# Silu and multiply kept in PSUM for the last tiles, adds on GpSimd, and GpSimd's and VectorE's remainders set apart in the load stage

## The chip, the cores and the metric

The kernel runs on one core of a Trainium2 chip. The metric is the time of the device in microseconds (us), the median of several runs; less is better. The profile is of one execution of the program. Its engines are PE (TensorE: matmuls, with PEld for its weight loads), DVE (VectorE), ACT (ScalarE), POOL (GpSimd) and SP, which here only issues DMAs.

## The reference

The input x has 2048 rows of 576. Two branches start from it and meet in the output.

```python
xn = _layernorm(x)
s  = A(xn)                 # linear attention, 32 heads of 18, hedgehog feature map
g  = _silu(B(xn))          # (silu(xn @ w_gate) * (xn @ w_up)) @ w_down, 4608 wide
return x + s * g
```

In A, q, k and v are xn times parts of `wqkv`; q and k are multiplied by `w_phi` per head and go through two softmaxes each (of the product and of its negative); `phi_k^T v` is summed over all rows, and each row of `phi_q` is multiplied by it, divided by its denominator and projected by `wo`. Everything is float32.

## The kernel before, in words

**Number format.** PE multiplies in a rounded 32-bit format (`F32R`). To keep accuracy, each operand is split in two: ACT rounds it (`hi`), and a subtraction gives the remainder (`lo = src - hi`). A product is then three matmuls, hi by hi, hi by lo, lo by hi. The width 576 is 4 x 128 + 64; the last 64 are kept as two tails of 32, each laid out so that the remainder of the tail lies in other partitions of the same tile as its rounded part. For x it is in partitions 32 to 63, for weights in 64 to 95; one matmul with 96 rows then does all three products of a tail. `split_rows` (L63) makes such a split of a weight: an ACT copy, a DVE subtraction for the two full chunks (L65) and a second one for the tail (L66).

**The load stage** (about the first 67 us) loads x in four blocks of 512 rows, in the order 2, 3, 0, 1. `norm_stats` (L179) takes mean and variance on DVE, with a square root on ACT. `norm_block` (L195) normalises the four 128-row pieces in turn on DVE (L201) and ACT (L198, collected in `norms`), copies the tails on POOL (L204), transposes on PE (L213), rounds the result into the `X` tiles on ACT (L215, L220) and subtracts for the remainders: the full chunks on DVE (L216), the two tails on POOL (L223), from a copy `xr` in SBUF (ACT, L221). `xr` also goes to DRAM from ACT's queue (L224). `fold` (L235) multiplies wk and later wq by w_phi on PE (L242) and splits the result into `KVWH`/`KVWL` and `QH`/`QL`. w_v comes in six chunks `wv[n]` with k = n // 3 and c = n % 3: ACT rounds each (L274), POOL subtracts for the four with c < 2 (L276, 128 x 576), DVE for the two tails c = 2 (L278, 32 x 576). The tiles `wst` that hold wk's five groups, w_v's six chunks and wq's five groups share five buffers, so SP's load of a later one waits until the one five places before it has been used. In between, `early_weights` (L102) splits the first weights of the feed-forward branch (ahead of other work, by `tc.high_priority()`) and `early_tile` (L119) computes gate and up products for the blocks that are ready, as work for PE: two PSUM banks `pe`, silu on ACT (L126), multiply on DVE (L130), store to DRAM, here from POOL's queue (L131).

**The middle** is k, v and the sums over rows, then q and the projection, then for both halves of the rows the feed-forward branch, whose gate and up products (L741) and down products (L866) are done by a seven-product scheme; `combine` (L1022) puts its sums together. For the first half the result goes to `y_dram` and is finished along the way (`late_finish`).

**The end** is `plain(1, ...)` (L869): the last two of the 36 column blocks of the feed-forward branch, added to the sums in `acc`, for the eight tiles of 128 rows of the second half, in the order 4, 5, 6, 7, 0, 1, 2, 3. For each tile `tile_of` (L882) fills a PSUM tile from `acc` on ACT (L893), adds 12 matmuls in two half widths of 288 (L866), and `finish` (L834) does silu on ACT into `acc` (L837), the multiply by s on DVE (L838), the add of x (L839) on DVE for even tiles and on POOL for odd ones, and the DMA to the output on SP (L840). s and x of two tiles at a time are loaded by `final_rows` (L854). Seven tiles use the two buffers `pd`, of two PSUM banks each; the last one, tile 3 (`fine`), uses the banks `py` and `pw`, one for each half, and finishes each half by itself, all on DVE. The other two banks, `px`, belong to the gate and up products and are idle here. So all eight banks are spoken for.

**What sets the order.** A scheduler orders each engine's instructions when the program is built: by their place in the text, by `tc.high_priority()`, and by its own model of when inputs are ready. `tc.issue_after(ins)` queues the instructions of a block behind `ins` in the queue of its engine. The engines work their queues in order.

Of the kernel before, what the change touches and what calls it, by code (L numbers as in the profile page):

```python
# [9 lines left out]
F32 = mybir.dt.float32  # L10
# [8 lines left out]
P = 128  # L19
# [29 lines left out]
def gated_hedgehog_kernel(ctx: ExitStack, tc, x, w_qk, w_v, w_phi, wo, w_gu, w_tail, w_down, ident_in, mask_in, out):  # L49
# [13 lines left out]
    def split_rows(hi, lo, src):  # L63
        nc.scalar.copy(hi, src)
        nc.vector.tensor_sub(lo, src[:, :, 0:2], hi[:, :, 0:2])  # L65
        nc.vector.tensor_sub(hi[64:96, :, 2], src[64:96, :, 2], hi[64:96, :, 2])  # L66
# [34 lines left out]

    def early_weights(f, *behind):  # L102
        parts = []
        for m in (0, 2):
            raw = epool.tile([P, 2, 3, P], F32, name="raw", bufs=2)
            hi = epool.tile([P, 2, 3, P], F32R, name="wh", bufs=3)
            lo = epool.tile([P, 2, 2, P], F32R, name="wl", bufs=3)
            nc.sync.dma_start(raw, w_gu[f, :, m:m + 2])
            with ExitStack() as order:
                for b in behind:  # L110
                    order.enter_context(tc.issue_after(b.ins))
                with tc.high_priority():
                    split_rows(hi, lo, raw)
            parts.append((hi, lo))
        return parts
# [19 lines left out]
    with ExitStack() as att:  # L135
# [17 lines left out]
        with ExitStack() as wst:  # L153
# [4 lines left out]
            with ExitStack() as pst:  # L158
# [36 lines left out]
                def norm_block(b, xns):  # L195
# [12 lines left out]
                    for c in range(3):  # L208
# [13 lines left out]
                        for m in range(2):  # L222
                            nc.gpsimd.tensor_sub(dst[m][32:64, 2], xr[32:64, m], dst[m][32:64, 2])  # L223
                            nc.scalar.dma_start(x_dram[i, :, :, 2 * j + m].rearrange("s p n -> p s n"),  # L224
                                                xr[:, m].rearrange("p (s n) -> p s n", s=4))
# [39 lines left out]
                wv = []  # L265
                for n in range(6):
                    wv.append(prep.tile([P, 6 * P], F32, name="wst", bufs=5))
                    nc.sync.dma_start(wv[n][:, 0:D], w_v[:, n // 3, n % 3])
                xns = load_x(0) + load_x(1)
                for n in range(6):  # L270
                    k, c = divmod(n, 3)
                    src, vh = wv[n][:, 0:D], KVWH[:, k, c, D:2 * D]
                    with tc.issue_after(copy.ins):
                        nc.scalar.copy(vh, src)  # L274
                    if c < 2:
                        nc.gpsimd.tensor_sub(KVWL[:, k, c, D:2 * D], src, vh)  # L276
                    else:
                        nc.vector.tensor_sub(vh[64:96], src[64:96], vh[64:96])  # L278
                wq = load_fold(1)
                norm_stats([0, 1], xns)  # L280
                norm_block(0, xns[0:4])
# [552 lines left out]
    def finish(t, k, pd, sx, eng):  # L834
        r0 = HS + t * P
        a = acc[:, t // 4 * 2:t // 4 * 2 + 2, t % 4][:, k]
        nc.scalar.activation(a, pd, AF.Silu)  # L837
        nc.vector.tensor_mul(a, a, halves_of(sx[:, 0])[:, k])  # L838
# [30 lines left out]
    def plain(i, fs, hr, final):  # L869
# [11 lines left out]

        def tile_of(t, hs):  # L882
            fine = i == 1 and t == HT // 2 - 1
            if fine:
                pd = [fps.tile([P, BT], F32, name=n, bufs=1)[:, 0:HALF] for n in ("py", "pw")]
            else:
                both = fps.tile([P, 2, 512], F32, name="pd", bufs=2)[:, :, 0:HALF]
                pd = [both[:, k] for k in range(2)]
            c = slice(t % 4 * P, t % 4 * P + P)
            a2 = acc[:, t // 4 * 2:t // 4 * 2 + 2, t % 4]  # L890
            with tc.high_priority() if i else ExitStack():
                for k in range(2 if fine else 1):
                    nc.scalar.copy(pd[k] if fine else both, a2[:, k] if fine else a2)  # L893
            for k in range(2):
# [3 lines left out]
                if fine:  # L898
                    finish(t, k, pd[k], final[t // 2][:, t % 2], nc.vector)
# [3 lines left out]
            elif not fine:  # L903
                finish(t, slice(0, 2), both, final[t // 2][:, t % 2], (nc.vector, nc.gpsimd)[t % 2])
# [250 lines left out]
```

## Time and profile before

| what | us |
|---|---|
| median of 3 runs (1623.53 to 1623.86) | 1623.55 |
| the profiled execution, its own time | 1622.04 |
| its span, first to last instruction | 1620.2 |
| PE busy in the span | 1605.8 (99%) |
| DVE busy | 1175.9 (73%) |
| ACT busy | 726.3 (45%) |
| POOL busy | 660.8 (41%) |

A row of the timeline gives the start in us from the span's beginning, how long the group took, the engine, the line of the kernel, the operation, what it writes and what it reads, the shape (partitions x elements) and how many instructions are merged in it; a bracket at the end says how long the engine had been idle before and what ended that. A row of a table by stage gives the stretch, its length, and for PE, PEld, DVE, ACT and POOL the busy time and the number of instructions; behind them stand the granted clock of PE, the share of DMA and GB/s. A row of the chain has start, length, engine, tile and line.

### The profile page before, as it was taken

The page shows a single profiled execution, that of the slowest core. Times are in us where ns is not written, and L with a number is a line of the kernel's source. Part 1 is how long each engine was busy: PE and PEld are TensorE (multiplying, and loading weights), DVE is VectorE, ACT ScalarE, POOL GpSimd, SP SyncE. Part 2 cuts the span into 40 slices and gives each one's busy share as a digit, 9 for nine tenths or more (in the row PEclk, how much of TensorE's full clock was granted, in tenths as well). Part 3 has the DMA queues.
Part 4 walks back from the last instruction along what each step waited for, and adds up shares of the span by engine and source line. Part 5 has one row for each costly group of instructions (what it writes and reads, how often), then busy time and mean ns, then how long its engine had stood idle before and what let it go on. Part 6 is the DMA issues. An engine that isn't in the chain of part 4 may idle for free.

```text
span 1620.2 us, 25277 instructions
## 1 busy us (share of the span) xinstructions
PE 1605.8 (99%) x9411; PEld 1428.2 (88%) x9412; DVE 1175.9 (73%) x1727; ACT 726.3 (45%) x1399; POOL 660.8 (41%) x710
## 2 busy tenths in 40 slices
PE   9999999999999999999999999999999999999998
PEld 6899998999988888888888888888888888888887
DVE  7777769898856778877777778634667656666578
ACT  5633345544445654444444444454343333333334
POOL 3676652334115635644535435223324314133132
PEclk9999999999999999999999999999999999999999
DMA  9522243436347454555545453965445654555435
GB/s 325 172 80 82 98 144 105 125 105 191 121 158 255 165 180 163 175 171 181 177 169 191 168 188 114 335 210 148 151 137 154 187 174 157 177 181 175 142 116 176
DMA packets 121420, 268.28 MB, mean 166 GB/s; under 512 B 12754, under 2 KB 53842, under 8 KB 119506
## 3 DMA queue, kind: packets, MB, share of 16 engines
q1 hardware_dynamic: 105852, 244.73, 45.9%
q0 software_dynamic: 3552, 12.59, 2.7%
q10 hardware_dynamic: 11894, 9.35, 1.8%
q8 instruction: 74, 1.21, 0.3%
q14 instruction: 48, 0.39, 0.1%
HBM read 167.53 MB, written 99.09 MB: 165 GB/s over the span
## 4 chain that ended last, share of the span: by engine, by line
PE 94%; DVE 3%; DMA 1%; ACT 1%; issue 0%; POOL 0%; SPq 0%; POOLq 0%; ACTq 0%
PE pd L866 25%; PE px L741 25%; PE pw L741 12%; PE p L94 7%; PE py L741 6%; PE pe L94 5%; PE p L641 4%; PE kvp L320 2%; PE po L621 2%; PE vx L408 1%; PE pt L615 1%; PE vw L408 1%; PE vy L94 1%; PE vx L94 1%; DVE stats L183 1%
## 5 line engine op out<-in xcount | busy, mean ns | idle before, releaser
L866 PEld LDWEIGHTS pd<-dw,hh 128*128 128x128 f32 x3036 | 431.0, 188 | 22.3 <-DVE X L997 0.9
L866 PE MATMUL pd<-dw,hh 128*128 128x288 f32 x3036 | 446.7, 297 | 0.7 <-DVE X L997 0.4
L741 PE MATMUL px<-X,w 128*128 128x512 f32 x1512 | 390.4, 393 | 0.0
L741 PEld LDWEIGHTS px<-X,w 128*128 128x128 f32 x1512 | 275.0, 188 | 52.7 <-ACT s L770 2.2
L741 PE MATMUL pw<-X,w 128*128 128x512 f32 x744 | 191.8, 393 | 0.0
L741 PEld LDWEIGHTS pw<-X,w 128*128 128x128 f32 x744 | 139.2, 189 | 30.9
L775 DVE TENSOR_TENSOR s<-pw,s 128x512 f32<-128x512 f32 x126 | 86.5, 688 | 101.0 <-ACT s L770 89.5
L997 DVE TENSOR_TENSOR acc<-pd,acc 128x576 f32<-128x576 f32 x128 | 96.2, 752 | 84.4 <-PE pd L866 84.2
L770 ACT COPY s<-px 128x512 f32<-128x512 f32 x126 | 73.9, 586 | 160.6 <-PE px L741 160.6
L61 DVE TENSOR_TENSOR hh<-ha,hh 128x512 fp32r<-128x512 f32 x140 | 111.9, 825 | 22.8 <-ACT hh L60 21.3
L60 ACT CAST hh<-ha 128x512 fp32r<-128x512 f32 x140 | 82.7, 619 | 87.0 <-PE pd L866 72.0
L969 POOL TENSOR_TENSOR hb<-hb 128x512 f32<-128x512 f32 x34 | 46.5, 1367 | 164.9 <-DVE hb L787 159.2
L94 PE MATMUL pe<-X,wh 128*128 128x512 f32 (+1 forms) x340 | 108.5, 399 | 1.9 <-POOL X L223 0.8
L61 DVE TENSOR_TENSOR w<-ld,w 128x512 fp32r<-128x512 f32 (+1 forms) x96 | 80.2, 835 | 36.6 <-ACT w L60 35.3
L741 PE MATMUL px<-X,wt 96*128 96x512 f32 x252 | 99.5, 395 | 0.0
L741 PE MATMUL py<-X,w 128*128 128x512 f32 x378 | 98.0, 394 | 0.0
L956 POOL TENSOR_TENSOR h<-ha,hb 128x512 f32<-128x512 f32 x34 | 44.4, 1305 | 125.1 <-DVE ha L791 95.2
L982 POOL TENSOR_TENSOR ha<-ha 128x512 f32<-128x512 f32 x34 | 52.6, 1563 | 98.7 <-DVE hh L61 98.7
L60 ACT CAST w<-ld 128x512 fp32r<-128x512 f32 (+1 forms) x96 | 52.7, 549 | 88.1 <-POOL ld L729 56.4
L795 ACT COPY py<-px 128x512 f32<-128x512 f32 x63 | 36.0, 572 | 106.4 <-PE px L741 83.4
L726 POOL TENSOR_TENSOR ts<-ld 128x256 f32<-128x256 f32 x32 | 27.4, 856 | 129.4 <-issue 73.3
L741 PEld LDWEIGHTS py<-X,w 128*128 128x128 f32 x378 | 67.8, 188 | 11.3
(275 smaller groups left out, 3249.2 us busy)
## 6 DMA issues: line engine op xcount, KB each, us to landing
w_dram<-w SPq DMA_DIRECT2D x90, 512.0 KB
w<-w_dram SPq DMA_DIRECT2D x90, 512.0 KB
wt<-t_dram SPq DMA_DIRECT2D x62, 336.0 KB
ld<-in_B_w_gu SPq DMA_DIRECT2D x32, 512.0 KB
X<-sum_dram SPq DMA_DIRECT2D x8, 1280.0 KB
rt<-in_B_w_down SPq DMA_DIRECT2D x33, 288.0 KB
rb<-in_B_w_down SPq DMA_DIRECT2D x33, 288.0 KB
w_dram<-w SPq DMA_DIRECT2D x30, 256.0 KB
```

What stands on the lines that cost most here:

```text
L60: nc.scalar.copy(hi, src)
L61: nc.vector.tensor_sub(lo, src, hi)
L94: last = nc.tensor.matmul(ps, l, r, start=n == 0, stop=n == len(pairs) - 1)
L641: nc.tensor.matmul(ps[:, 0:HALF], a[0:w, g, jc], bw[0:w, g, n], start=k == 0, stop=k == 3 * NG - 1)
L741: nc.tensor.matmul(ps, l, r, start=first and n == 0, stop=last and n == len(mm) - 1, skip_group_check=True)
L770: snaps.append(nc.scalar.copy(t, ps))
L775: nc.vector.tensor_add(t, ps, t)
L866: nc.tensor.matmul(ps, l, r, start=first and n == 0 and m == 0, stop=n == len(hs) - 1 and m == 2, skip_group_check=True)
L956: sub(s, g["h"][0][0], g["h"][0][1])
L969: nc.gpsimd.tensor_add(a21, a21, g["h"][1][1])
L982: sub(a12, a12, g["h"][0][0])
L997: nc.vector.tensor_add(a2, pd[:, :, 0:HALF], a2)
```

## The change

There are two parts.

In the load stage the two tail remainders of block 3 (the second block loaded) move from POOL to DVE with high priority and read PSUM. w_v's chunks are loaded and treated in another order: the four with c < 2 first, their POOL subtractions under `issue_after` of the last subtraction of the early weights (`rests[-1]`); the two tails c = 2 come in the text only behind the norms of block 0, their DVE subtractions under `issue_after` of `norms[5]`. The load of wq comes behind them in the text.

At the end `finish` is cut in two. `scaled` does the silu within PSUM and multiplies from PSUM into `acc`; `finish` adds x and stores. The adds go to POOL for all tiles but the last. Tiles 6 and 1 (`apart`) use the two `px` banks, one for each half, and are multiplied, added and stored by halves. For those two and the last tile, the fills are queued behind the tile before's, and the adds behind the second half's multiply.

```diff
     def split_rows(hi, lo, src):
...
-        nc.vector.tensor_sub(hi[64:96, :, 2], src[64:96, :, 2], hi[64:96, :, 2])
+        return nc.vector.tensor_sub(hi[64:96, :, 2], src[64:96, :, 2], hi[64:96, :, 2])
...
+    rests = []
+
     def early_weights(f, *behind):
...
-                    split_rows(hi, lo, raw)
+                    rests.append(split_rows(hi, lo, raw))
...
                         for m in range(2):
-                            nc.gpsimd.tensor_sub(dst[m][32:64, 2], xr[32:64, m], dst[m][32:64, 2])
+                            if b == 3:
+                                with tc.high_priority():
+                                    nc.vector.tensor_sub(dst[m][32:64, 2], ps[32:64, m], dst[m][32:64, 2])
+                            else:
+                                nc.gpsimd.tensor_sub(dst[m][32:64, 2], xr[32:64, m], dst[m][32:64, 2])
...
-                wv = []
-                for n in range(6):
-                    wv.append(prep.tile([P, 6 * P], F32, name="wst", bufs=5))
-                    nc.sync.dma_start(wv[n][:, 0:D], w_v[:, n // 3, n % 3])
+                wv, places = [], [(0, 0), (0, 1), (1, 0), (1, 1), (0, 2), (1, 2)]
+                for k, c in places:
+                    wv.append(prep.tile([P, 6 * P], F32, name="wst", bufs=5)[:, 0:D])
+                    nc.sync.dma_start(wv[-1], w_v[:, k, c])
                 xns = load_x(0) + load_x(1)
-                for n in range(6):
-                    k, c = divmod(n, 3)
-                    src, vh = wv[n][:, 0:D], KVWH[:, k, c, D:2 * D]
+                for (k, c), src in zip(places[0:4], wv):
+                    vh = KVWH[:, k, c, D:2 * D]
                     with tc.issue_after(copy.ins):
                         nc.scalar.copy(vh, src)
-                    if c < 2:
+                    with tc.issue_after(rests[-1].ins):
                         nc.gpsimd.tensor_sub(KVWL[:, k, c, D:2 * D], src, vh)
-                    else:
+                norm_stats([0, 1], xns)
+                norm_block(0, xns[0:4])
+                for (k, c), src in zip(places[4:6], wv[4:6]):
+                    vh = KVWH[:, k, c, D:2 * D]
+                    with tc.issue_after(copy.ins):
+                        nc.scalar.copy(vh, src)
+                    with tc.issue_after(norms[5].ins):
                         nc.vector.tensor_sub(vh[64:96], src[64:96], vh[64:96])
                 wq = load_fold(1)
-                norm_stats([0, 1], xns)
-                norm_block(0, xns[0:4])
...
-    def finish(t, k, pd, sx, eng):
+    def scaled(t, k, pd, sx):
+        a = acc[:, t // 4 * 2:t // 4 * 2 + 2, t % 4][:, k]
+        nc.scalar.activation(pd, pd, AF.Silu)
+        return nc.vector.tensor_mul(a, pd, halves_of(sx[:, 0])[:, k])
+
+    def finish(t, k, sx, eng):
         r0 = HS + t * P
         a = acc[:, t // 4 * 2:t // 4 * 2 + 2, t % 4][:, k]
-        nc.scalar.activation(a, pd, AF.Silu)
-        nc.vector.tensor_mul(a, a, halves_of(sx[:, 0])[:, k])
         eng.tensor_add(a, a, halves_of(sx[:, 1])[:, k])
...
+        fills = []
+
         def tile_of(t, hs):
             fine = i == 1 and t == HT // 2 - 1
+            apart = fine or (i == 1 and t in (HT // 2 + 2, 1))
             if fine:
                 pd = [fps.tile([P, BT], F32, name=n, bufs=1)[:, 0:HALF] for n in ("py", "pw")]
+            elif apart:
+                pd = [fps.tile([P, BT], F32, name="px", bufs=2)[:, 0:HALF] for _ in range(2)]
...
             with tc.high_priority() if i else ExitStack():
-                for k in range(2 if fine else 1):
-                    nc.scalar.copy(pd[k] if fine else both, a2[:, k] if fine else a2)
+                for k in range(2 if apart else 1):
+                    with tc.issue_after(fills[-1].ins) if apart else ExitStack():
+                        last = nc.scalar.copy(pd[k] if apart else both, a2[:, k] if apart else a2)
+            fills.append(last)
...
-                if fine:
-                    finish(t, k, pd[k], final[t // 2][:, t % 2], nc.vector)
+                if apart:
+                    done = scaled(t, k, pd[k], final[t // 2][:, t % 2])
+            if apart:
+                with tc.issue_after(done.ins):
+                    for k in range(2):
+                        finish(t, k, final[t // 2][:, t % 2], nc.vector if fine else nc.gpsimd)
...
-            elif not fine:
-                finish(t, slice(0, 2), both, final[t // 2][:, t % 2], (nc.vector, nc.gpsimd)[t % 2])
+            elif not apart:
+                scaled(t, slice(0, 2), both, final[t // 2][:, t % 2])
+                finish(t, slice(0, 2), final[t // 2][:, t % 2], nc.gpsimd)
```

## The prediction, made before the changed kernel was run

> **What bounds the kernel now.** I read the first and fourth parts of the page, then the stage table of TensorE (PE), then PE's idle rows, then the rows of the engines that those waits name.
>
> ```profile
> PE 1605.8 (99%) x9411; PEld 1428.2 (88%) x9412; DVE 1175.9 (73%) x1727; ACT 726.3 (45%) x1399; POOL 660.8 (41%) x710
> PE 94%; DVE 3%; DMA 1%; ACT 1%; issue 0%; POOL 0%; SPq 0%; POOLq 0%; ACTq 0%
> 48.47:67.33 18.86, 18.72 (x136) 17.10 (x137) 12.74 (x19) 15.30 (x22) 7.94 (x19) 1.00 0.59 208
> 67.33:230.00 162.67, 162.67 (x1259) 159.97 (x1258) 116.95 (x151) 61.66 (x155) 115.22 (x115) 1.00 0.26 85
> ```
>
> PE works 1605.8 of 1620.2 us, so all its idle time is 14.4 us, and no edit that leaves the matmuls alone can gain more. The two stretches (length, then busy time of PE first) show that from 48.47 us on PE has a full queue. What starts earlier there ends earlier by the same amount: a gain of the load stage is carried through. The change touches two places where PE does wait. The first is the load stage; these are PE's rows there, the bracket being the idle time before and what ended it.
>
> ```profile
> 35.50 0.73 PE L94 MATMUL pe<-X,wh 96*128 96x512 f32 x2 [0.83 <-POOL X L223]
> 44.11 0.47 PE L94 MATMUL pe<-X,wh 128*128 128x512 f32 x1 [0.82 <-DVE h L130]
> 48.47 0.87 PE L213 MATMUL tp<-ident,xn 128*128 128x128 f32 x3 [0.85 <-DVE xn L201]
> ```
>
> Together 0.83 + 0.82 + 0.85 = 2.50 us: the most the load stage can give. The second and third wait for VectorE (DVE), which works nearly without a pause up to the normalised rows `xn`. Why is it late? Four of its remainders take far longer than their twins:
>
> ```profile
> 19.40 1.37 DVE L65 TENSOR_TENSOR wl<-raw,wh 128x512 fp32r<-128x512 f32 x2
> 20.78 0.75 DVE L66 TENSOR_TENSOR wh<-raw,wh 32x256 fp32r<-32x256 f32 x2
> 34.18 2.96 POOL L223 TENSOR_TENSOR X<-xr,X 32x512 fp32r<-32x512 f32 x2
> 34.57 1.43 DVE L65 TENSOR_TENSOR wl<-raw,wh 128x512 fp32r<-128x512 f32 x1
> 36.03 1.39 DVE L66 TENSOR_TENSOR wh<-raw,wh 32x256 fp32r<-32x256 f32 x1
> 39.70 3.27 POOL L276 TENSOR_TENSOR KVWL<-wst,KVWH 128x576 fp32r<-128x576 f32 x2 [0.96 <-ACT KVWH L274]
> 39.78 1.91 DVE L65 TENSOR_TENSOR wl<-raw,wh 128x512 fp32r<-128x512 f32 x1
> 41.72 1.53 DVE L66 TENSOR_TENSOR wh<-raw,wh 32x256 fp32r<-32x256 f32 x1
> ```
>
> Quiet, L65 takes 1.37 / 2 = 0.69 and L66 0.75 / 2 = 0.38. Beside GpSimd (POOL) L223 the same pair takes 1.43 + 1.39, which is 1.75 too much; beside L276 it takes 1.91 + 1.53, 2.37 too much. Not every DVE operation suffers:
>
> ```profile
> 1594.11 3.12 POOL L1034 TENSOR_TENSOR acc<-acc,X 128x1152 f32<-128x1152 f32 x1 [3.83 <-DVE acc L997]
> 1595.33 0.75 DVE L997 TENSOR_TENSOR acc<-pd,acc 128x576 f32<-128x576 f32 x1
> ```
>
> L997 has one input in PSUM and runs its usual 0.75 inside a POOL operation. So the victims are those with both inputs in SBUF. [...]
>
> The second place is the end, after PE's last matmul:
>
> ```profile
> 1605.50 1.43 POOL L839 TENSOR_TENSOR acc<-acc,X 128x576 f32<-128x576 f32 x1 [8.26 <-DVE acc L838]
> 1608.25 0.75 DVE L838 TENSOR_TENSOR acc<-acc,X 128x576 f32<-128x576 f32 x1
> 1605.96 1.58 DVE L838 TENSOR_TENSOR acc<-acc,X 128x576 f32<-128x576 f32 x1 [0.54 <-ACT acc L837]
> 1611.81 0.95 PE L866 MATMUL pw<-dw,hh 128*128 128x288 f32 x6
> 1612.73 1.91 POOL L839 TENSOR_TENSOR acc<-acc,X 128x576 f32<-128x576 f32 x1 [2.21 <-issue]
> 1612.80 0.41 ACT L837 ACTIVATE acc<-pw 128x288 f32<-128x288 f32 x1
> 1613.30 1.65 DVE L838 TENSOR_TENSOR acc<-acc,X 128x288 f32<-128x288 f32 x1
> 1615.91 0.45 DVE L838 TENSOR_TENSOR acc<-acc,X 128x288 f32<-128x288 f32 x1
> 1616.39 0.46 DVE L839 TENSOR_TENSOR acc<-acc,X 128x288 f32<-128x288 f32 x1
> ```
>
> PE ends at 1611.81 + 0.95 = 1612.76, the last silu at 1613.21, but the last add only at 1616.85: DVE is behind, and a half-width multiply (0.45 quiet) takes 1.65 beside POOL's add. From 1616.85 to the end at 1620.2 is the last output's DMA, 3.35 us, which the change leaves.
>
> **The change part by part: load stage.** (1) Block 3's two tail remainders leave POOL (1.5 us each, not on PE's path but for the 0.83) and come to DVE, which is on the path. No row shows a 32x512 one on DVE: it lies between L66's 0.38 (32 partitions, 256 columns) and the 0.69 of L65's 512 columns. The columns are what sets a duration here, so I take 0.69, twice: +1.38. In exchange L223 no longer lies beside the first L65 and L66: -1.75. PE's tail matmuls then wait for DVE, not for the copy `xr` and POOL. (2) Of the six w_v chunks, both DVE ones (L278) go behind the norms in the text:
>
> ```profile
> 44.00 0.75 DVE L278 TENSOR_TENSOR KVWH<-wst,KVWH 32x576 fp32r<-32x576 f32 x1
> 46.83 0.20 DVE L189 RECIPROCAL rs<-rs 128x8 f32<-128x8 f32 x1 [0.28 <-ACT rs L188]
> ```
>
> The first of them stood in DVE's chain ahead of the last statistics: -0.75. If the scheduler drops it into the gap at 46.83, where DVE waits for the square root, it costs 0.75 - 0.28 = 0.47 again, so -0.28 is the weak end. The buffers of the two chunks come free later, and the wq loads behind them on SP's queue with them. Those now feed the fold's fourth and fifth groups:
>
> ```profile
> 54.98 5.52 PE L242 MATMUL tp<-PHI,wst 126*128 126x126 f32 x48
> 61.04 1.46 PE L242 MATMUL tp<-PHI,wst 72*128 72x72 f32 x12
> ```
>
> Twelve matmuls are a group, so PE needs them at 54.98 + 36 x 0.115 = 59.1 and at 61.0; the chunks should be free by about 52, behind the norms, which covers a load of several us. Without that cover PE would wait for it, 1 us for 1. (3) The four POOL subtractions L276 carry `issue_after` of a DVE operation. That construct orders instructions within one engine's queue and makes no wait between engines; every block under it in the old kernel holds an operation of that engine. So I expect it to hold nothing, and likewise the `norms[5]` one (ACT against DVE). L276 depends on ACT's casts as before, and so stays beside the second L65 and L66: 0.
>
> Sum for DVE: 1.38 - 1.75 - 0.75 = -1.1 us, so the rows reach PE 1.1 earlier, within the 2.50 that PE has to give. Bounds: with L278 in the gap -0.65 and some order lost, -0.3; with the L276 contention gone too, -3.5, cut by PE to -2.5. If L276 instead takes L223's place beside the first pair, +1.38 - 0.75 = +0.6. I take **-1.1**.
>
> **The end.** (4) The silu stays in PSUM and DVE multiplies from there. Durations:
>
> ```profile
> 1597.27 0.69 DVE L787 TENSOR_TENSOR hb<-px,s 128x512 f32<-128x512 f32 x1 [1.19 <-ACT px L786]
> 1596.65 0.58 ACT L786 ACTIVATE px<-px 128x512 f32<-128x512 f32 x1 [1.96 <-PE px L741]
> 1602.35 0.64 ACT L893 COPY pd<-acc 128x576 f32<-128x576 f32 x1
> 1605.37 6.48 PE pd L866 x48
> ```
>
> L786 and L787 are this very pair at 512 columns, and L997 is the 576 one: 0.75, no dearer than L838's quiet 0.75 from SBUF, and not stretched by POOL. So the seven muls shrink from 0.75 to 1.8 down to 0.75. [...]
>
> (5) The adds of all seven whole tiles go to POOL. PE makes a tile in 6.48 / 4 = 1.62 us, POOL adds one in 1.43, and a tile in halves takes twice the 0.80 of the first row here:
>
> ```profile
> 70.89 0.80 POOL L374 TENSOR_TENSOR raw<-sraw 128x288 f32<-128x288 f32 x1
> 1601.94 1.35 DVE L1035 TENSOR_TENSOR acc<-acc,X 128x1152 f32<-128x1152 f32 x1
> ```
>
> The first multiply follows the second row, DVE's, at 1603.3, and ends at 1604.0. From there that is 5 x 1.43 + 4 x 0.80 = 10.4 of work: POOL is done between 1614.4 and 1615.1, its last add following the multiply of the tile before last at about 1613. (6) The last tile: its fills are now ordered behind those of the seventh tile, so PE loses a filler:
>
> ```profile
> 1600.91 1.09 PE L866 MATMUL py<-dw,hh 128*128 128x288 f32 x4
> 1601.84 2.34 PE L866 MATMUL pd<-dw,hh 128*128 128x288 f32 x16
> ```
>
> Four matmuls of py ran while the second pd was awaited; now they run at the end, up to 4 x 0.135 = 0.54, less what ACT saves by not filling py first (0.40): I take +0.3 on PE's end, 1613.06. Then silu 0.41, multiply 0.45, both adds 0.91, hops of about 0.05: 1615.0. The adds have two SBUF inputs, and POOL's last add is running until 1614.4 to 1615.1; a wait of up to 0.5 gives 1615.5. Against 1616.85: **-1.3**, bounds -1.9 (no wait, no lost filler) and -0.5 (both in full, and the two adds one behind the other's DMA on SP). (7) The px banks: a pd pair is now held through PE 1.62, silu 0.65, multiply 0.75, fill 0.64 and hops, 3.9 us. Two pairs alone give PE 2 x 1.62 = 3.24; with px as the third, 4.86. So no wait, by 1.0 us: 0. DVE's cover for that is that it has only 0.75 per tile to do.
>
> **Sum.** -1.1 - 1.3 = -2.4 us. The profiled execution took 1622.04 us (span 1620.2), 1.5 under the median of 1623.55; the difference carries over: 1623.55 - 2.4 = 1621.1 us, -0.15%.
>
> **Rivals.** (a) *The second pair is relieved too* (the scheduler puts L276 later, or L65 and L66 ahead of it): DVE gains 3.5, PE gives its full 2.5, in all -3.8: 1619.8. For it: L65 and L66 have high priority, and the ACT cast in front of the second pair stood behind a silu that waited for PE, which waited for L223:
>
> ```profile
> 37.19 0.19 PEld L94 LDWEIGHTS pe<-X,wh 96*128 96x128 f32 x1 [0.24 <-POOL X L223]
> 37.73 0.60 ACT L126 ACTIVATE h<-pe 128x512 f32<-128x512 f32 x1 [0.55 <-PE pe L94]
> ```
>
>  Against: statistics stand before them and POOL starts at ACT's casts as before. (b) *The gain is half lost*: POOL's adds take 1.91 as at 1612.73, not 1.43, and POOL ends at 1604.0 + 7 x 1.91 = 1617.4, so the end loses 0.5; or the load stage gives nothing and the end alone -1.3. 1622.2 to 1623.0. (c) *The ring stalls PE: slower*. If the px fills, ordered behind the fill before them, come too late, two pd pairs turn alone: each turn lacks 3.9 - 3.24 = 0.65, two turns 1.3, the first more by the 0.9 from the silu's end (1602.35, where the fill row above starts) to L1035's end, for which its multiply waits, and the filler 0.54: PE ends 2.7 late. After PE there remain 2.4 instead of 4.1, so the end comes 1.0 later; with the load stage's +0.6, 1625.2. It decides once a fill starts over 1.0 us after its turn. Against it: ACT has 1.3 us of work for each 1.62 of PE. (d) *The holds hold nothing*: that is in the forecast; if they did hold, it is (a).
>
> **How the numbers follow.** Forecast 0.47 (own range 1620.1 to 1622.2), (a) 0.25, (b) 0.18, (c) 0.10. The range for 8 in 10 reaches from (a)'s lower side, 1618.9, to the upper side of (b), 1624.2, and leaves most of (c) out. A change of 0.2%, 3.25 us, is about what a measurement of this kernel can tell from none: faster by that needs 1620.3 or less, nearly all of (a) and a little of the forecast, 0.27; slower needs 1626.8, the far part of (c), 0.07; the rest 0.66.
>
> **What would show it.** L65 and L66 of the first pair at 0.69 and 0.38, the second still near 1.9 and 1.5; the new subtractions near 0.69; PE's three idle rows shrunk by 1.1 in sum; the multiplies at 0.75 throughout; POOL's last add ending near 1615, DVE's near 1615.5, PE's last matmul near 1613 on the old clock. I am wrong if PE waits for ACT's fills in the last 15 us, if the second pair is quiet, or if the order in the middle stages changes enough to move the rest of PE's 14.4 us of idle time.

## The result and the profile after

| | median, us | runs | lowest to highest |
|---|---|---|---|
| before, on the same chip | 1623.5 | 17 | 1621.88 to 1624.93 |
| changed | 1626.43 | 17 | 1624.21 to 1629.18 |

The ratio is 1.002, 95% interval 1.0012 to 1.0027: the changed kernel is 2.9 us slower (1.9 to 4.4). 2.4 less was forecast, so the forecast missed by 5.3. The profiled executions, 1622.04 and 1627.26, lie 5.2 apart, more than the medians: single executions differ by a microsecond or two (the last `xn` row of the first two blocks starts at 27.85 in before's execution and at 29.88 in that of e1, which has the same load stage). So below a wait or a duration is read from a profile, but a gain or a loss from the medians. The profile of one experiment, e9, was taken at a granted clock of 0.752 and is not read; its time stands.

First the rows of PE in which it waits, and the rows around the new one, of the changed kernel's timeline. The bracket is the idle time and what ended it.

```profile
50.19 1.31 PE L215 MATMUL tp<-ident,xn 128*128 128x128 f32 x7 [1.22 <-DVE xn L203]
51.72 2.44 PE L215 MATMUL tp<-ident,xn 128*128 128x128 f32 x17 [0.22 <-POOL xn L206]
66.76 1.36 PE L215 MATMUL tp<-ident,xn 128*128 128x128 f32 x11
70.25 0.40 PE L94 MATMUL p<-KVWH,X 128*128 128x288 f32 x1 [2.12 <-ACT xr L223]
1606.83 1.85 PE L878 MATMUL pd<-dw,hh 128*128 128x288 f32 x12 [1.33 <-ACT pd L911]
```

The two early waits of 0.83 and 0.82 are gone. The one for `xn` grew from 0.85 to 1.22 + 0.22 in this execution, and there are two new ones: 2.12 at the first k product, which waits for the copy `xr` of the last transposed chunk, and 1.33 in the end. In the chain that ended last, the k block behind the first of these is longer than its twins of the same 28 matmuls:

```profile
70.25 5.51 PE p L94 x28
79.49 3.73 PE p L94 x28
89.01 3.73 PE p L94 x28
```

1.78 us is lost there. Of it 0.27 is paid at full clock too: in e4, e5, e13 and e14 below, where this block starts behind a wait of 0.18 to 0.34, it takes 4.00 at a granted clock of 1.00. The other 1.51 goes beyond that, and the table by stage (its last three columns are the granted clock, the share of DMA and GB/s) says where it comes from:

```profile
68.00:72.00 4.00, 1.88 (x11) 1.75 (x10) 1.60 (x6) 3.01 (x5) 1.71 (x2) 0.86 0.35 111
72.00:76.00 4.00, 4.00 (x25) 4.00 (x23) 0.20 (x1) 0.47 (x1) 3.76 (x5) 0.72 0.25 71
```

PE is never idle from 72 to 76, but its granted clock is 0.72. So the wait costs twice: 2.12 + 1.78 = 3.9 us, more than the whole change lost (2.9).

Next DVE's chain in the load stage, and POOL's subtractions beside it:

```profile
35.32 1.28 DVE L227 TENSOR_TENSOR X<-tp,X 32x512 fp32r<-32x512 f32 x2
36.63 0.69 DVE L65 TENSOR_TENSOR wl<-raw,wh 128x512 fp32r<-128x512 f32 x1
37.36 1.54 DVE L66 TENSOR_TENSOR wh<-raw,wh 32x256 fp32r<-32x256 f32 x1
40.89 1.30 DVE L65 TENSOR_TENSOR wl<-raw,wh 128x512 fp32r<-128x512 f32 x1
42.94 0.81 DVE L66 TENSOR_TENSOR wh<-raw,wh 32x256 fp32r<-32x256 f32 x1
45.94 0.75 DVE L289 TENSOR_TENSOR KVWH<-wst,KVWH 32x576 fp32r<-32x576 f32 x1
47.16 0.75 DVE L289 TENSOR_TENSOR KVWH<-wst,KVWH 32x576 fp32r<-32x576 f32 x1
47.95 0.69 DVE L132 TENSOR_TENSOR h<-pe,h 128x512 f32<-128x512 f32 x1
48.55 0.19 DVE L191 RECIPROCAL rs<-rs 128x8 f32<-128x8 f32 x1
37.13 6.35 POOL L281 TENSOR_TENSOR KVWL<-wst,KVWH 128x576 fp32r<-128x576 f32 x4 [1.94 <-ACT KVWH L279]
```

Both c = 2 remainders (L289) stand ahead of the reciprocal for the norms, behind which they were to be held. The four L281 run without a pause from 37.13. In before the first of them, at 37.31, lay beside statistics, since DVE's first pair came 2.1 us earlier, and the next two met the second pair. Here the first one meets the first pair's L66 (1.54), and the second pair is half relieved. That meeting differs from execution to execution: e2, e3, e4, e5 and e13 below have the same load stage up to this row (but for the ring in e5 and e13), and L66 took 1.68 in e2's but 0.42 in the other four, as here in e5's:

```profile
37.64 0.42 DVE L66 TENSOR_TENSOR wh<-raw,wh 32x256 fp32r<-32x256 f32 x1
```

From the last `xn` row of the first two blocks to the first one of the other two DVE takes 19.90 to 19.92 in the five executions with the load stage of before (before, e1, e8, e10, e14). With the changed one it takes 20.55 (the changed kernel), 20.63 (e2), 20.22 (e5) and 19.39 to 19.52 (e3, e4, e13). PE's wait at the first of these transposes goes with it: 1.22, 1.27, 0.92, and 0.23 or none. What decides this length stays open; the size of this wait in one execution says little. The 2.12 at the k product is the same in all three executions that have it (the changed kernel, e2, e11).

At the end, DVE's multiplies, its last adds, POOL's adds, and the last three outputs that SP issues:

```profile
1615.38 0.76 DVE L846 TENSOR_TENSOR acc<-pd,X 128x576 f32<-128x576 f32 x1 [1.98 <-ACT pd L845]
1616.22 4.57 POOL L851 TENSOR_TENSOR acc<-acc,X 128x576 f32<-128x576 f32 x4 [1.31 <-DVE acc L846]
1617.29 0.96 PE L878 MATMUL pw<-dw,hh 128*128 128x288 f32 x6
1617.42 0.76 DVE L846 TENSOR_TENSOR acc<-pd,X 128x576 f32<-128x576 f32 x1 [0.55 <-ACT pd L845]
1618.10 0.45 DVE L846 TENSOR_TENSOR acc<-py,X 128x288 f32<-128x288 f32 x1
1619.09 2.02 DVE L851 TENSOR_TENSOR acc<-acc,X 128x288 f32<-128x288 f32 x2
1620.82 1.70 SPq L852 DMA_DIRECT2D out<-acc  x3
```

From PE's end (1618.25) to the last add (1621.11) are 2.86 us; before it was 1616.85 - 1612.76 = 4.09. That part did gain 1.2. In this execution most of it is lost again on SP: its queue has the output of POOL's last tile ahead of the last tile's, POOL's last add ends at 1620.79, and the last three outputs go out from 1620.82 on. From the last add to the end of the span are 1625.4 - 1621.11 = 4.29, where before had 3.35 (in e1 it is 3.87). So from PE's end to the end of the span it is 7.15 instead of 7.44, a gain of 0.3 (0.7 in e1), and PE's wait of 1.33 ahead of it takes more than that.

### The profile page after: what moved, and what is told of

Same layout as the page of the kernel before. It is cut to its first block, busy times and chain, and to the rows that moved or that the text cites. A ratio compares the mean times of both kernels' runs of the same rounds, so it can differ in the third digit from the quotient of the medians.

```text
span 1625.4 us, 25284 instructions
## 1 busy us (share of the span) xinstructions
PE 1607.5 (99%) x9412; PEld 1430.1 (88%) x9412; DVE 1170.6 (72%) x1727; ACT 726.7 (45%) x1403; POOL 664.4 (41%) x714
## 4 chain that ended last, share of the span: by engine, by line
PE 96%; DMA 2%; DVE 1%; ACT 0%; issue 0%; DVEq 0%; POOL 0%; SPq 0%; ACTq 0%; POOLq 0%
PE px L750 25%; PE pd L878 25%; PE pw L750 12%; PE p L94 7%; PE pe L94 6%; PE py L750 6%; PE p L650 4%; PE kvp L329 2%; PE po L630 2%; PE vx L417 1%; PE pt L624 1%; PE vw L417 1%; PE tp L248 1%; PE vy L94 1%; PE vx L94 1%; DMA raw<-in_B_w_gu 0%
```

## The experiments

**Theory.** In the load stage the time goes to a clash of PSUM banks. (The traces do not name banks. These, and the order of the chunks, are read from the built programs; the runs with a turned ring test what follows from them.) The tiles `tp` go round in three slots of two banks (0-1, 2-3, 4-5), and the k product's tile comes later in banks 0-1. In the built program of before, the last transposed chunk lies in 4-5, and banks 0-1 come free two chunks earlier. In the changed one the scheduler takes two chunks of a block in another order, the last chunk ends in 0-1, and the k product must wait until ACT has copied it. PE has nothing in hand there: having waited less earlier, it has used up the early tiles' matmuls, of which before still had eight behind the last transposes. The idle time then lowers the clock (0.72 from 72 to 76). In the end, the time goes to fills that ACT's queue has behind a silu. **Rivals:** the new order of w_v's loads is dear by itself; the end is what lost; the wait alone, without the clock, is the loss.

**e1_tail_only, e2_load_only: one half each.** Each undoes one half of the change, as the text of before has it.

```diff
# e1: the changed kernel without the load stage's part
-                            if b == 3:
-                                with tc.high_priority():
-                                    nc.vector.tensor_sub(dst[m][32:64, 2], ps[32:64, m], dst[m][32:64, 2])
-                            else:
...
-                wv, places = [], [(0, 0), (0, 1), (1, 0), (1, 1), (0, 2), (1, 2)]
...
# e2: the changed kernel without the end's part
-            apart = fine or (i == 1 and t in (HT // 2 + 2, 1))
...
-                scaled(t, slice(0, 2), both, final[t // 2][:, t % 2])
...
```

> Only the end of the kernel is changed; the load stage is that of before. Theory A (from the profile after): the fill of the second last tile in pd stands behind the first tile's silu in ScalarE's queue, so TensorE waits 1.33 us there, and the last adds wait for GpSimd's: the end costs 0.5 to 1.0 us, 1624.0 to 1624.5 where before is 1623.5. Rival (my prediction): it gains 1.3 us, 1622.2.

> Only the load stage is changed; the end is that of before. Theory A: TensorE is out of work after the last transposes, the first k product waits 2.1 us for the copy xr to leave its PSUM banks, and then runs at about half the clock for 4 us (1.6 us lost): 2 to 3.7 us slower than before, 1625.5 to 1627.2. Rival (my prediction): 1.1 us faster, 1622.4. If the loss of the whole change came from the end, this would be within 0.5 us of before.

Measured: e1 1623.33 (before 1623.34), ratio 1.0002, 0.9993 to 1.001; e2 1625.42, ratio 1.0012, 1.0003 to 1.0021. The loss is the load stage's, +2.1; the end gives nothing that can be told from none (-1.1 to +1.6 us). In e1's timeline PE has the end's wait alone, in e2's the k product's:

```profile
1604.25 1.85 PE L869 MATMUL pd<-dw,hh 128*128 128x288 f32 x12 [1.33 <-ACT pd L902]
```

e2:

```profile
50.21 1.31 PE L215 MATMUL tp<-ident,xn 128*128 128x128 f32 x7 [1.27 <-DVE xn L203]
51.74 3.84 PE L215 MATMUL tp<-ident,xn 128*128 128x128 f32 x17 [0.22 <-POOL xn L206]
71.68 0.40 PE L94 MATMUL p<-KVWH,X 128*128 128x288 f32 x1 [2.12 <-ACT xr L223]
```

In e2's execution the wait for `xn` too was followed by a low clock: 17 transposes took 3.84 instead of 2.44.

**e3_load_banks, e4_load_dummies: the clash away, or the idle time filled.** Both are e2 with one more edit. e3 allocates v's and kvp's banks ahead, so that the k product's tile gets banks 6-7; e4 leaves the clash and puts nine matmuls on zeros behind the last transposes.

```diff
# e3
+            for n in ("vx", "vy", "vw"):
+                kps.tile([P, 512], F32, name=n)
+            kvp = [kps.tile([GW, 4, GW + 1], F32, name=f"kvp{i}") for i in range(3)]
...
# e4
-                norm_block(1, xns[4:8])
+                last, _, _ = norm_block(1, xns[4:8])
...
+                spent = eps.tile([P, BT], F32, name="pe")
+                with tc.issue_after(last.ins):
+                    for _ in range(9):
+                        nc.tensor.matmul(spent, idle[:, 0:P], idle, start=True, stop=True)
```

> As e2, but the k product's tile p2 gets the two PSUM banks that the early tiles use, by allocating the v tiles and the sums ahead of it; nothing else is changed. Theory A: no wait at about 68 us and no slow clock, so 3.5 us less than e2 (at least 2), 1622 to 1624. Rival B: the first k product would wait anyway, for the weights or the x blocks (the chain of norms and casts is the bound, whatever the banks): then within 0.5 us of e2.

> As e2, with nine matmuls of zeros of 512 columns (2 us) queued on TensorE behind the last transposes; they compute nothing that is used. Theory A: the wait for the banks stays, so the first k product starts at the same time as in e2 (within 0.3 us), but the clock stays granted and its 28 matmuls take 3.7 us instead of 5.4: 1.6 us less than e2. Rival C (the half speed comes from the weights or x arriving late, not from the clock): no change, or 0.3 us more.

Measured: e3 1623.79, ratio 1.0, 0.9992 to 1.0009; e4 1624.36, ratio 1.0009, 1.0 to 1.0018. In e3's timeline, the first row behind the transposes and a later one:

```profile
67.79 0.38 PE L94 MATMUL p<-KVWH,X 128*128 128x288 f32 x1
...
226.14 0.40 PE L94 MATMUL p<-QH,X 128*128 128x288 f32 x1 [0.87 <-ACT zb L544]
```

The wait is gone, but other tiles got other banks too, and a wait of 0.87 came up at the first q product: by the medians e3 is 1.6 under e2, where at least 2 was expected. e4's timeline:

```profile
66.67 2.11 PE L298 MATMUL pe<-idle 128*128 128x512 bf16 x9
68.95 0.40 PE L94 MATMUL p<-KVWH,X 128*128 128x288 f32 x1 [0.18 <-ACT xr L223]
```

and its stage table:

```profile
72.00:76.00 4.00, 4.00 (x33) 4.00 (x32) 2.94 (x4) 0.69 (x1) 3.84 (x6) 1.00 0.00 0
```

The product starts as late after the transposes as with the wait, but PE was busy, and the clock stays at 1.00: the 28 matmuls take 4.00 instead of e2's 5.52. e4 gains 1.1 on e2 by its median, where 1.6 was expected; the intervals overlap.

**e5_load_ring, e6_load_held_ring: the ring turned, and a hold that holds.** Both start from e2. Two of the 28 idle matmuls at the start write to `tp` tiles, so that the ring stands two slots further; the work is the same. e6 also names an operation of the same engine in the hold: `scales` collects the normalising operations of L203.

```diff
-                keep_clock(28)
+                keep_clock(26)
+                for _ in range(2):
+                    turn = pps.tile([P, 2, BT], F32, name="tp", bufs=3)
+                    nc.tensor.matmul(turn[:, 0], idle[:, 0:P], idle, start=True, stop=True)
# e6 besides
...
-                    with tc.issue_after(norms[5].ins):
+                    with tc.issue_after(scales[5].ins):
```

> The changed load stage with the end of before, and two of the 28 idle matmuls at the start write to tiles of the ring of the transposes, so that the ring is two turns further: the last transposed chunk then lies in banks 2 and 3, and banks 0 and 1, which the first k product takes, come free with the chunk two before it. The work is the same. Theory (bank clash): the first k product starts right behind the transposes (wait under 0.4 us instead of 2.12), the granted clock of the k block stays above 0.95 (instead of 0.57), and no other bank changes places, so the 0.87 us wait that e3 had at the first q product is not there: 1622.9 us (1622.4 to 1623.4), 2.5 under e2. Rival (the new order of the w_v loads and remainders is dear by itself, through its DMAs or the engines): the wait moves elsewhere and the time stays at 1624.5 or more.

> e5, and the hold of the two c=2 remainders names an operation of the same engine (VectorE's scaling of the row tile, not ScalarE's), so that it holds. Theory (a hold that names another engine's operation holds nothing): the two remainders of 0.75 us leave VectorE's chain ahead of the normalised rows, PE's wait of 1.22 us at the first transposes of blocks 0 and 1 shrinks to under 0.3, and the time is 1.0 to 1.3 under e5: 1621.7 us. Rival (the chain is bound by the loads or the statistics, not by these remainders): the wait stays above 0.8 and the time within 0.4 of e5.

Measured: e5 1622.06 (before 1623.93), ratio 0.9996, 0.9987 to 1.0004; e6 1621.66, ratio 0.999, 0.9981 to 0.9999. PE's waits in e5's and in e6's timeline:

```profile
50.16 1.31 PE L215 MATMUL tp<-ident,xn 128*128 128x128 f32 x7 [0.92 <-DVE xn L203]
68.44 0.40 PE L94 MATMUL p<-KVWH,X 128*128 128x288 f32 x1 [0.34 <-DVE X L218]
```

e6:

```profile
48.06 0.87 PE L215 MATMUL tp<-ident,xn 128*128 128x128 f32 x5 [0.57 <-DVE xn L203]
```

e5 takes back all that the load stage lost (0.0016 of ratio against e2, 2.6 us). In e6 both remainders stand behind the first norms, so here the hold works: DVE's stretch up to the norms is 18.23 instead of e5's 20.22, and the rows reach PE 2.1 us earlier. But PE's wait for them is 0.57, where under 0.3 was expected. By these two executions PE's idle time shrinks only by 0.92 - 0.57 here and by the 0.34 at the k product, 0.69 in all: the rest of the 2.1 us was not idle time but early-tile matmuls, which PE now still has in hand behind the transposes. What counts is PE's idle time, not when the rows come. And this wait varies: it is 0.23 in e13, which has e5's load stage, and 0.32 and 0.71 in e12 and e15, which have e6's. The time falls by 0.4 (median) to 1.0 (ratio), with intervals that overlap, so the gain of the hold over e5 is not shown.

**e7_order_alone, e11_tails_alone: which half of the load stage's part.** Before with only w_v's new order and holds (e7); before with only block 3's tails on DVE (e11), where the ring again ends in banks 0-1.

```diff
# e11: all that is changed of before
-                            nc.gpsimd.tensor_sub(dst[m][32:64, 2], xr[32:64, m], dst[m][32:64, 2])
+                            if b == 3:
+                                with tc.high_priority():
+                                    nc.vector.tensor_sub(dst[m][32:64, 2], ps[32:64, m], dst[m][32:64, 2])
+                            else:
+                                nc.gpsimd.tensor_sub(dst[m][32:64, 2], xr[32:64, m], dst[m][32:64, 2])
```

> Before, with the new order of the six w_v chunks and both holds alone; block 3's tail remainders stay with GpSimd. Here the ring stands as in before (last chunk in banks 4 and 5, the k product's banks free early). Theory (the moved tail remainders alone change the order of the chunks in the ring and so the banks): no wait at the first k product, the two early waits of 0.8 stay, one of the two c=2 remainders still stands ahead of the norms: 1623.3 us, within 0.5 of before. Rival (the later w_v chunks hold up buffers, loads or VectorE): 1624.5 or more, with a wait at the transposes above 1.2 us or at the fold.

> Before, with block 3's two tail remainders on VectorE and nothing else of the change. Here the ring of the transposes ends in banks 0 and 1, as in the changed kernel. Theory (this part alone brings the wait at the first k product): PE's two early waits of 0.8 are gone, the first k product waits about 2.1 us for the copy of the last transposed chunk, the block behind it runs at a granted clock under 0.7 for some 4 us, and the time is 1.5 to 2.1 above before: 1625.2 us. Rival (the wait needs the new order of the w_v chunks as well): the first k product starts within 0.4 us, and the time is 0.8 to 1.6 under before.

Measured: e7 1623.05 (before 1623.93), ratio 1.0, 0.9991 to 1.0009; e11 1628.52 in five runs (before 1623.41), ratio 1.0032, 1.002 to 1.0044. No cost of the loads' order shows. The tails bring the clash, and more than expected. Two rows of e11's timeline:

```profile
50.40 1.31 PE L213 MATMUL tp<-ident,xn 128*128 128x128 f32 x7 [1.62 <-DVE xn L201]
71.72 0.40 PE L94 MATMUL p<-KVWH,X 128*128 128x288 f32 x1 [2.12 <-ACT xr L221]
```

and two of its stage table:

```profile
52.00:56.00 4.00, 4.00 (x20) 3.62 (x21) 0.98 (x1) 2.91 (x4) 2.95 (x13) 0.62 0.65 267
72.00:76.00 4.00, 4.00 (x20) 4.00 (x20) 0.00 (x0) 1.28 (x1) 3.84 (x5) 0.57 0.48 131
```

Two waits, and a low clock behind each. The wait for `xn`, 1.62, costs 1.25 more by the clock (the 17 transposes behind it took 3.69), as in e2's execution; that second loss the expectation had left out. In this execution one w_v remainder on DVE took 2.38, beside POOL's, where its twin in before takes 0.75 (L278); that can account for the long wait.

**e13_after_ring, e14_before_ring: is the clash enough, is it needed?** The same two matmuls in the ring, in the whole changed kernel (e13), where they take the clash away, and in before (e14), where they bring it.

> The changed kernel, with nothing else than the two idle matmuls in the ring of the transposes, as in e5. Theory (the change's loss is the bank clash at the first k product with the cold clock behind it): the wait of 2.12 us is under 0.4, the k block runs at a granted clock over 0.95, and the time is 1622.5 to 1623.2, that is 3.2 to 3.9 under the changed kernel and 0.2 to 1.0 under before; the end still has its wait of 1.33. Rival (something else in the change costs the 2.9 us): 1625 or more.

> The kernel before, with two idle matmuls in the ring, which here turn it the wrong way: the last transposed chunk now lies in banks 0 and 1, which the first k product takes. The eight matmuls of the early tile still stand behind the last transposes (1.86 us). Theory (the wait needs the clash and an empty queue together): the first k product waits 0.2 to 0.5 us, the clock stays at 1.00, and the time is 0.2 to 0.5 above before, 1623.7. Rival (the clash alone is enough): a wait over 1 us, a clock under 0.8 behind it, and 1625 or more.

Measured: e13 1622.84, ratio 0.9998, 0.9988 to 1.0007; e14 1624.17, ratio 1.0003, 0.9994 to 1.0012 (before 1623.73). e14's timeline:

```profile
67.08 0.64 PE L94 MATMUL pe<-X,wh 128*128 128x512 f32 x2
67.97 0.40 PE L94 MATMUL p<-KVWH,X 128*128 128x288 f32 x1 [0.26 <-ACT xr L221]
```

Without the clash the changed kernel is 3.6 us faster by the ratios. The profiles put 3.29 on it: the wait and the k block took 2.12 + 5.51 in the changed kernel and 0.34 + 4.00 in e13. And before bears the same clash with a wait of 0.26, as it still has early-tile matmuls behind the transposes. Both are needed: the clash and the empty queue.

**e8_tail_rot, e9_tail_free, e10_tail_rot_free: the end's wait.** All on the load stage of before. e8 gives `px` to the sixth and the first tile; e9 no longer holds py's and pw's fills; e10 does both.

```diff
# e8, e10
-            apart = fine or (i == 1 and t in (HT // 2 + 2, 1))
+            apart = fine or (i == 1 and t in (HT // 2 + 1, 0))
# e9, e10
-                    with tc.issue_after(fills[-1].ins) if apart else ExitStack():
+                    with tc.issue_after(fills[-1].ins) if apart and not fine else ExitStack():
```

> Load stage of before, end of the change, but the two whole tiles on px are the sixth and the first of the half (5 and 0) instead of 6 and 1. The sixth tile's fill then needs no pd pair that the fourth tile's silu still holds. Theory (PE's wait of 1.33 us in the end comes from the fill that stands in ScalarE's queue behind the silu of the tile two before it): the wait falls under 0.4, PE ends 1.0 to 1.3 earlier against its 9300th matmul, and the time is 1.0 to 1.3 under e1's 1623.33: 1622.1 us. Rival (ScalarE's queue is full in these 15 us whatever the banks): a wait of 1 us or more at the next fill, and the time within 0.4 of e1.

> e1 (load stage of before, end of the change), but the fills of the last tile's two banks, py and pw, are no longer ordered behind the seventh tile's fills; all else of the end is the change's. Theory (holding these fills back costs more than the four py matmuls of filler: without them ScalarE takes the silu of the fourth tile first and the next pd fill after it, and PE has nothing for 1.33 us): four py matmuls run again before the last whole tiles, the pd fill stands ahead of the silu in ScalarE's queue, PE's wait falls from 1.33 to under 0.4, PE ends about 1.0 to 1.3 earlier against its 9300th matmul, and the time is 1622.3 us against e1's 1623.33. Rival (the pd bank itself comes free too late, since VectorE's multiply now reads it): the wait stays above 0.9 and the time within 0.4 of e1.

> e8 (px for the sixth and the first tile) with py and pw fills not held. By the theory of e9 PE has six py and four pw matmuls, 10 x 0.135 = 1.35 us, as filler for the wait of 1.33 that e8 kept before its fourth tile, and only two pw matmuls (0.3) are left behind the last whole tile instead of twelve: PE's wait under 0.3, and what follows PE's end is longer, since the last whole tile's silu, multiply and add then stand behind it (0.65 + 0.76 + 1.43 on GpSimd against 0.40 + 0.46 + 0.9): 7.4 to 7.8 us after PE's end instead of 6.7. Sum -1.3 + 0.9: 1622.6 us. Rival (the wait stays): 1623.9.

Measured: e8 1622.99 (before 1623.93), ratio 0.9998, 0.999 to 1.0007; e9 1623.15 (before 1623.41), ratio 0.9998, 0.9989 to 1.0007; e10 1623.01, ratio 0.9996, 0.9987 to 1.0005. None differs measurably from before, and none shows the 1.0 us or more under e1 that was expected of e8 and e9. In e8 the wait, which was to fall under 0.4, only moved:

```profile
1604.52 0.75 DVE L837 TENSOR_TENSOR acc<-pd,X 128x576 f32<-128x576 f32 x1
1605.67 0.64 ACT L836 ACTIVATE pd<-pd 128x576 f32<-128x576 f32 x1 [1.26 <-PE pd L869]
1606.22 0.64 ACT L902 COPY pd<-acc 128x576 f32<-128x576 f32 x1
1606.91 1.86 PE L869 MATMUL pd<-dw,hh 128*128 128x288 f32 x12 [1.33 <-ACT pd L902]
```

This names it more exactly than the expectation did. The pd bank had been free since DVE's multiply ended at 1605.27, and ACT was idle; but its queue had the silu of the tile just computed first, and that waited for PE. So PE idles for a silu and a fill. In e10 the same two rows stand at 1606.16 and 1606.71, but ten py and pw matmuls run meanwhile, and PE has no wait over 0.17 in the end.

**e12_both_rot_free, e15_both_free: both mended.** e6's load stage with the end of e10, and with that of e9.

> The load stage of e6 (ring turned, hold on the same engine) with the end of e10 (px for the sixth and the first tile, py and pw not held). If the two places are independent, as PE's full queue between them says: e6's ratio 0.9990 times e10's 0.9996 (with e1's end as the middle term between), so 0.9986 of before, 1621.1 us where before has 1623.4. Rival (what the load stage gains is given back between the stages, or the end's gain lies under the last output's DMA): 1622.5 or more.

> The load stage of e6 with the end of e9 (the change's end, py and pw fills not held). Theory (the held fills cost PE its filler and the order of ScalarE's queue): four py matmuls run while the second pd bank is awaited, the pd fill stands ahead of the silu, PE's wait under 0.4 instead of 1.33, and what follows PE's end about 6.7 us as in e1: 1620.6 to 1621.2 us. Rival (the pd banks come free too late, since VectorE's multiply behind its long addition of the halves reads them): a wait of 0.9 us or more, and 1621.7 or more.

Measured: e12 1620.4, ratio 0.9981, 0.9972 to 0.9989; e15 1619.85, ratio 0.9978, 0.9969 to 0.9988 (before 1623.73). Both beat both kernels; e15 by 3.6 us against before. Its end, PE and ACT:

```profile
1599.02 1.09 PE L881 MATMUL py<-dw,hh 128*128 128x288 f32 x4
1599.95 1.81 PE L881 MATMUL pd<-dw,hh 128*128 128x288 f32 x12
...
1599.21 0.64 ACT L914 COPY pd<-acc 128x576 f32<-128x576 f32 x1
1599.79 0.73 ACT L914 COPY px<-acc 128x288 f32<-128x288 f32 x2
1600.46 0.61 ACT L848 ACTIVATE pd<-pd 128x576 f32<-128x576 f32 x1
```

The fill stands ahead of the silu, and four py matmuls bridge what is left. The gains of e6 and e9, 0.0010 and 0.0002, do not quite add to e15's 0.0022, but the intervals (each 0.0009 to either side) allow it; how much of e15 is the end's is open.

## Why the prediction was wrong, step by step

- **The step that failed: "from 48.47 us on PE has a full queue. What starts earlier there ends earlier by the same amount".** PE's queue was empty at 68.1, and what it waited for is no part of the change: a PSUM slot that the scheduler had dealt out differently. In before PE had eight early-tile matmuls left behind the last transposes, and e14 shows that these cover the clash; that PE had them because it had waited 1.65 us earlier on is read from the timelines, not tested. The wait and the low clock behind it, 3.9 us, were a term that the sum did not have. The last sentence of the prediction named a change of order in the middle stages as a way to be wrong, but gave it no chance or price.
- **(1) The tails on DVE.** 0.64 each where 0.69 was taken. The pairs' contention fell by (2.82 - 2.23) + (3.44 - 2.11) = 1.92; 1.75 was forecast, all of it on the first pair. That the sum fits is luck: 0.59 came off the first pair and 1.33 off the second, and where the first pair was quiet (e3, e4, e5, e13) it fell by 2.7 to 3.1. Which remainders suffer depends on which meet POOL's.
- **(2) The c = 2 remainders leave DVE's chain: wrong in sign.** Not -0.75 but +0.75, less the 0.28 of DVE's gap that one of them fills: the second one joined the first, and L132's 0.69 came ahead of the norms too. For DVE's chain as a whole -1.1 was forecast. It was +0.65 in the changed kernel's execution (20.55 against 19.90), and from -0.5 to +0.7 in the six executions with this load stage.
- **PE's three idle rows** were to shrink by 1.1 in sum. They went from 2.50 to 1.22 + 0.22, by 1.06. That is luck too: two were gone, the third grew, and in e13 the same rows left 0.23 + 0.22.
- **(3) The holds hold nothing: right**, but its consequence was not drawn for (2): the hold that does nothing was the one that should have kept L289 back. In e6, where it names the same engine, both stand behind the first norms.
- **(4) Multiplies from PSUM: right**, 0.76 and 0.45, none stretched, also beside POOL's adds (0.76 at 1612.64, within three that run from 1610.29 to 1613.27): a whole tile takes 0.75 from SBUF in before, where it is quiet, and 0.75 to 0.76 from PSUM here.
- **(5) POOL's adds: right in duration** (1.43 for a tile), but they came late, since the multiplies waited for silus that stood behind fills (1.98 at 1615.38); the last ones still met DVE's (2.02 for two that take 0.9 quiet). That the 3.35 us behind the last add stay was wrong: they became 4.29, since POOL's late last add held back the outputs in SP's queue. The bound of -1.9, said to be without the lost filler, still has it in: without it the end would come at 1614.7, 2.2 earlier.
- **(6) The held fills: mis-sized.** +0.3 was taken for the lost filler; the runs with the hold (the changed kernel, e1, e8, e13) have a wait of 1.33 or 1.34, because without the early py fill ACT's queue also has the silu ahead of the next fill.
- **(7) The px ring: right**, no wait at px.
- **The rivals.** (c) had the right kind of cause for the end, PE waiting for a fill in ACT's queue, which the prediction also named as a sign of being wrong; but it was a pd fill, not one of px, and with 1.33 half of the 2.7 in size. In (a), the second pair was relieved in part. No rival had a loss in the load stage through another tile.

## What to carry to other kernels

Taking a wait out of a filled pipeline can spend the filler early: before counting the gain, look at what the engine has in hand at the next point where it depends on others, and which PSUM slot the next stage's first tile shares with whose last reader. A change to one engine's work can turn the rotation of a tile ring, so compare slots between the two built programs, not only instructions. And a hold is worth something only on the engine that works the held queue (18.23 up to the norms in e6, where it names an operation of that engine, 20.22 in e5, where it does not).

## What the runs showed of the hardware

In five places of these runs a short idle time of PE cost 0.7 to 1.1 times as much again by the clock. Idle times of 2.12 (the changed kernel, e2, e11), 1.62 (e11) and 1.27 (e2) were followed by some 4 us at a granted clock of 0.57 to 0.72. The matmuls behind them took 1.25 to 1.52 us longer than the same ones at a clock of 1.00. Idle times of 1.22 (the changed kernel at 50 us), 0.92 (e5) and 0.85 (before) were not: the clock is 1.00 from 48 to 56 in all three. Nor was the wait in the end, 1.33 or 1.34 in the four executions that have it (the changed kernel, e1, e8, e13): the 12 matmuls behind it take 1.85 or 1.86 in each, and the granted clock is 1.00 around it in e1 (1604 to 1608) and in the changed kernel:

```profile
1606.00:1610.00 4.00, 3.17 (x24) 3.17 (x24) 2.94 (x4) 2.66 (x7) 1.43 (x1) 1.00 0.04 12
```

That is the changed kernel's stage table around its wait of 1.33. So length alone doesn't decide; what else counts wasn't tried and stays open. That the single runs of e2 (1622.84 to 1627.84) and of the changed kernel spread by 5 us, and before's by 3, may come from the `xn` wait: it is 0 to 1.27 in the six executions with this load stage, and a low clock followed the 1.27 but not the 1.22. This is argued, not shown.
